# A new planned order for the first 430 operations, with a page model for TensorE's instructions

## The chip, the cores and the metric

The kernel runs on one core of one Trainium2 chip. The metric is device microseconds of one execution, lower is better. Engines are named as the profile names them: PE is TensorE (PEld its weight loads), DVE VectorE, ACT ScalarE, POOL GpSimd, SP SyncE.

## The reference

Two stages, in float32. Attention: for each of 24 chunks of 32 queries, softmax over 8 memory keys and a window of 56 keys, for 4 batches and 8 heads of 64. Then a gated block on x (4 x 768 x 512):

```python
scores = scale * np.matmul(q_c, k_full.transpose(0, 1, 3, 2))   # q_c 32 x 64, k_full 64 x 64
a = np.exp(scores - np.max(scores, axis=-1, keepdims=True))
out[:, :, c_start:c_end] = np.matmul(a / (np.sum(a, -1, keepdims=True) + 1e-09), v_full)
...
h = np.maximum(x @ w_in, 0.0)                  # 512 -> 1024
u, v = h[..., :512], h[..., 512:]
v_n = (v - mean(v)) / np.sqrt(var(v) + 1e-06)
v_s = np.einsum('ts,bsd->btd', w_spatial, v_n) + b_spatial[None, :, None]
out = (u * v_s) @ w_out
```

## The kernel before

The work is cut into 24 attention units of 4 chunks (128 queries, all 8 heads), six to a batch, and into matmul groups of the gated block. A unit i has a burst of small products on PE, `burst`: 64 for the scores and 64 for the weighted values of unit i-1. For units 0 to 3 these are two bursts of 64 (scores, tile sx; values, tile f), from unit 4 on one burst of 128. `softmax` runs on DVE and ACT: `mx` (maximum), `p` (subtraction, then exp), `den`, `rec`. `flip` turns the probabilities (tile pt, copied to pT) and the unit's result xs (tile xt, copied to x); up to unit 8 that is done by PE. `prep` copies the halo of the keys (k from k), before a unit's scores may start.

The gated block's groups (`group`, the matmuls of L901) accumulate in a ring of four PSUM tiles f. Each float32 product is three fp32r products of high and low parts. `ffn_v` and `ffn_u` multiply x by the two halves of w_in, `spatial` by w_spatial (needs the normalised `vn` of all six units of a batch), `ffn_o` by w_out.

w_in and w_out arrive as float64 words. `from_f64` turns each of 12 blocks (8 of w_in, 4 of w_out) into float32 and then into high and low parts, in seven operations: `scale_` (ACT or POOL, L1085 or L1087), `shift` (DVE, L1095), `sign` (DVE, L1101), `high` (ACT or POOL, L386), `rest` (ACT, L1091), `add` (POOL, L1106), `low` (DVE or POOL, L1113).

The order is made by the program itself at build time. Every call of `op` adds an operation with a number, its engine (or a price for each of several engines), its reads and writes and a rank. `Plan.order` is a list scheduler: it walks simulated time, and on each engine takes the operation with the smallest

```python
c = (late + ops[n][10], ops[n][4], n)     # start time + wait, rank, number
```

The table `ORDER` changes single operations by number: (added to the rank, wait, the one engine allowed or ''). Each engine then executes its operations in exactly the planned order, and an operation that waits holds up all behind it on its engine. The loads of SP stand in a queue of their own whose order is that of the list `FIRST` and of the calls; each may start only after the one before it (`after=line`), and at most `AHEAD` bytes of loads are under way.

The table's numbers run in the order of the calls: 0 to 107 are the first loads and the blocks of w_in (14 to 20 block (1,1), 22 block (0,1), 36 block (2,1)); 108 to 117 are unit 0 (110 its `mx`), 133 the key copy of unit 2, 242 to 273 the four blocks of w_out, 274 to 379 `ffn_v` and `ffn_u` of batch 0, and 384 to 429 units 7 to 9 in part.

## Time and profile before

| | us |
|---|---|
| median of 3 runs (lowest, highest) | 381.64 (380.35, 385.66) |
| the profiled execution, its own time | 381.86 |
| its span in the trace | 379.6 |

The span runs from the first to the last instruction that the trace shows; 2.26 us of the execution lie outside it. All rows of the trace below are from that one execution, and their times count from the start of its span. A busy time of PE counts pipelined matmuls, so that neighbours overlap in it.

### The profile page before, as it was taken

Reading aid. Unit: us, or ns where it says so; the run is one execution under the profiler, and the core shown is the slowest. Engines: PE = TensorE matmul, PEld = TensorE weight load, DVE = VectorE, ACT = ScalarE, POOL = GpSimd, SP = SyncE. Lnnn points to the kernel's source line nnn. Section 1 sums busy time; section 2 is a strip of 40 time slices with the busy share of each in tenths; the row PEclk is TensorE's granted clock in tenths of the full one; section 3 lists DMA queues with packets and bytes.
Section 4 is the critical chain, followed back from the end, with each engine's and each line's share of the span. In section 5 each row is a group of like instructions: output and inputs, shape, how many; then the busy total and the mean of one; then the engine's idle time right before and its main releaser. Section 6 shows DMA issues by size and latency. Waiting matters only on the chain.

```text
span 379.6 us, 11226 instructions
## 1 busy us (share of the span) xinstructions
PE 356.5 (94%) x4692; PEld 319.1 (84%) x4692; DVE 204.6 (54%) x408; ACT 253.5 (67%) x659; POOL 151.1 (40%) x230
## 2 busy tenths in 40 slices
PE   1486999989999999999999999999999999999996
PEld 0364898979899889899899889899898889999995
DVE  0777868866437275765546274764555362603030
ACT  4885997862676977877975977879776983411112
POOL 4784786556434323434624323304514410213031
PEclk9999999999999999999999999999999999999999
DMA  6989735971023153134122352124120100000202
GB/s 217 287 301 244 283 98 154 293 233 58 3 86 130 72 147 76 50 79 152 41 87 80 146 126 75 48 60 162 51 86 2 55 29 2 1 0 3 83 0 85
DMA packets 29243, 39.71 MB, mean 105 GB/s; under 512 B 5192, under 2 KB 23304, under 8 KB 29192
## 3 DMA queue, kind: packets, MB, share of 16 engines
q1 hardware_dynamic: 28968, 38.91, 32.7%
q8 instruction: 37, 0.61, 0.7%
q14 instruction: 14, 0.11, 0.1%
q10 hardware_dynamic: 224, 0.08, 0.1%
HBM read 32.69 MB, written 6.29 MB: 103 GB/s over the span
## 4 chain that ended last, share of the span: by engine, by line
PE 82%; ACT 6%; DVE 4%; issue 3%; POOL 2%; DMA 2%; SPq 0%; POOLq 0%; ACTq 0%
PE f L901 71%; PE sx L629 7%; ACT xs L719 2%; POOL st L1087 2%; ACT pT L386 2%; DMA big<-in_moe_w_in_dram 2%; PE pt L818 1%; PE xt L845 1%; PE f L629 1%; DVE mx L743 1%; DVE p L747 1%; ACT big L1020 1%; ACT p L762 1%; DVE vn L963 1%; DVE st L1101 0%
## 5 line engine op out<-in xcount | busy, mean ns | idle before, releaser
L901 PE MATMUL f<-wsp_h,vn 128*128 128x384 f32 x384 | 99.1, 339 | 0.0
L901 PE MATMUL f<-x,win_h 128*128 128x384 f32 x256 | 72.7, 341 | 0.0
L901 PEld LDWEIGHTS f<-wsp_h,vn 128*128 128x128 f32 x384 | 69.3, 188 | 2.6
L901 PE MATMUL f<-wout,big 128*128 128x512 f32 (+1 forms) x300 | 71.4, 382 | 0.0
L901 PE MATMUL f<-wsp_l,vn 128*128 128x384 f32 x192 | 64.5, 336 | 0.0
L719 ACT COPY xs<-sx 32x128 f32<-32x128 f32 x240 | 61.6, 257 | 3.3 <-PE sx L629 0.4
L901 PE MATMUL f<-win_h,x 128*128 128x512 f32 x192 | 63.3, 411 | 0.5 <-ACT x L851 0.2
L901 PEld LDWEIGHTS f<-wout,big 128*128 128x128 f32 x300 | 54.3, 188 | 9.1
L1017 POOL TENSOR_TENSOR st<-st,u 128x384 f32<-128x384 f32 x32 | 33.4, 1044 | 66.2 <-DVE st L1013 45.4
L901 PEld LDWEIGHTS f<-x,win_h 128*128 128x128 f32 x256 | 47.0, 188 | 1.4
L944 POOL TENSOR_TENSOR rstd<-ve,mhalf 128x1 f32<-128x1 f32 x24 | 15.2, 636 | 73.6 <-DVE ve L940 64.5
L386 ACT COPY pT<-p 32x128 f32<-32x128 f32 x144 | 42.6, 296 | 2.3 <-POOL p L798 0.5
L901 PE MATMUL f<-x,win_l 128*128 128x384 f32 x128 | 43.3, 338 | 0.0
L901 PEld LDWEIGHTS f<-win_h,x 128*128 128x128 f32 x192 | 35.4, 193 | 7.7 <-DVE x L855 0.5
L1020 ACT CAST big<-st 128x384 fp32r<-128x384 f32 x32 | 16.4, 512 | 35.8 <-POOL st L1017 35.4
L1013 DVE TENSOR_TENSOR st<-f,bias 128x384 f32<-128x384 f32 x32 | 17.8, 556 | 39.2 <-PE f L901 38.8
L901 PE MATMUL f<-win_l,x 128*128 128x512 f32 x96 | 38.5, 401 | 0.0
L901 PEld LDWEIGHTS f<-wsp_l,vn 128*128 128x128 f32 x192 | 36.1, 188 | 0.0
L1024 DVE TENSOR_TENSOR big<-st,big 128x384 fp32r<-128x384 f32 x32 | 19.4, 605 | 24.8 <-ACT big L1020 24.8
L798 POOL TENSOR_TENSOR p<-p,rec 128x512 f32<-128x512 f32 x15 | 15.7, 1044 | 40.2 <-DVE rec L775 40.2
L386 POOL COPY pT<-p 32x128 f32<-32x128 f32 x96 | 29.8, 310 | 4.4
L629 PEld LDWEIGHTS sx<-k,q 64*32 64x32 f32 x1536 | 17.4, 110 | 14.3 <-POOL k L386 7.9
(91 smaller groups left out, 511.6 us busy)
## 6 DMA issues: line engine op xcount, KB each, us to landing
out_dram<-st SPq DMA_DIRECT2D x23, 256.0 KB
k<-in_k_dram SPq DMA_DIRECT2D x7, 800.0 KB
q<-in_q_dram SPq DMA_DIRECT2D x7, 768.0 KB
vmain<-in_v_dram SPq DMA_DIRECT2D x38, 128.0 KB
vmain<-in_v_dram SPq DMA_DIRECT2D x37, 96.0 KB
big<-in_moe_w_spatial_dram SPq DMA_DIRECT2D x6, 384.0 KB
big<-in_moe_w_in_dram SPq DMA_DIRECT2D x4, 512.0 KB
stage_w<-in_moe_w_in_dram SPq DMA_DIRECT2D x4, 512.0 KB
```

The source lines that it names most:

```text
L386: return (nc.scalar.copy if e == "ACT" else nc.gpsimd.tensor_copy)(o, a).ins
L629: nc.tensor.matmul(o, w_, m, start=start, stop=True, skip_group_check=True)
L719: last_ = (nc.scalar.copy if e == "ACT" else nc.vector.tensor_copy)(o, a).ins
L743: nc.vector.tensor_reduce(mx, s, axis=AX.X, op=ALU.max)
L798: (nc.vector if e == "DVE" else nc.gpsimd).tensor_tensor(p3, p3, rec, op=ALU.mult)
L901: return [nc.tensor.matmul(o, ll if x == 1 else lh, rl if x == 2 else rh, start=x == j == 0, stop=j == len(pairs) - 1 and x == (single[-1] ...
L944: nc.gpsimd.tensor_tensor(a, t_["ve", i], mhalf, op=ALU.pow)
L1013: nc.vector.tensor_tensor(alloc("st", s_, [P, HT], F32), t_["f", n], bias[:, tok], op=ALU.add)
L1017: nc.gpsimd.tensor_tensor(a, a, t_["u", i], op=ALU.mult)
L1020: nc.scalar.copy(t_["g", i][:, 0, 0:HT], t_["st", s_])
L1024: nc.vector.tensor_tensor(a[:, 1, 0:HT], t_["st", s_], a[:, 0, 0:HT].bitcast(F32), op=ALU.subtract)
L1087: nc.gpsimd.tensor_scalar(o, a, 2.0 ** -112, None, op0=ALU.mult)
```

## The change

No operation of the computation is added or taken away. What changes is the order in which the engines execute them, on which of two engines some of them run, and 18 small products that PE executes at the start, into a PSUM tile that nothing reads (`PADS`). The new order follows from four things:

- `ORDER` has 370 entries, for operations 0 to 429, where it had 72 for 5 to 323.
- POOL's prices for `scale_` and `high` of `from_f64` go from 0.75 and 0.7 to 1.5 and 1.0 us.
- A class `Pages` takes the place of the page count: the first matmul instruction is number 67 + 4 x `PADS` in its page, a few instructions in a hundred or a thousand are added to the count, PE's queue is sent up to `DEPTH` instructions ahead of their start, and page n+1 is there `FETCH` after the later of `ASK` past the entry of page n and the landing of the last load begun by then.
- The readiness of an operation by engines other than PE (`others`) limits when its instructions are sent.

The diff, its table cut to lines that the text below speaks of:

```diff
 ORDER = {
-    5: (0, 0, 'ACT'), 6: (21, 3, 'ACT'), 8: (34, 1.5, 'POOL'), 9: (46, 0.4, 'ACT'), 19: (-32, 3, ''),
-    20: (-34, 3, 'DVE'), 22: (22, 0, 'POOL'), 28: (19, 0, 'POOL'), 40: (-20, 0, ''), 48: (27, 0, 'ACT'),
...
+    11: (0, 0.8, ''), 12: (20.6, 0, ''), 13: (-19.7, 0, ''), 14: (36, 0, ''), 15: (26.5, 0.8, ''),
+    16: (12.7, 0.4, ''), 17: (16.5, 0, ''), 18: (9, 0.4, ''), 19: (5.9, 0, ''), 20: (10.7, 6, ''),
+    21: (24.5, 0.8, ''), 22: (40.1, 3, 'POOL'), 23: (-4.6, 0, ''), 24: (-30.7, 0, ''), 25: (77.8, 0, ''),
...
+    34: (-67.3, 6, ''), 35: (70.3, 0.2, ''), 36: (-13.8, 0, 'ACT'), 37: (54.9, 0, ''), 39: (21.1, 0, 'ACT'),
...
+    109: (-20.3, 0.4, ''), 110: (-36.1, 0, ''), 111: (-83.4, 0, ''), 112: (70, 0.4, ''), 113: (-70.7, 0, ''),
...
+    130: (-16.9, 0, ''), 131: (10.6, 0, ''), 132: (61.2, 0.4, ''), 133: (128.8, 0.4, ''), 134: (53.2, 0, ''),
...
+    239: (35.7, 0, ''), 241: (23.6, 0, ''), 242: (-1.8, 0.8, ''), 243: (-46.7, 0, 'ACT'), 244: (-141.6, 0, ''),
+    245: (-14.5, 0, ''), 246: (-59, 0, 'ACT'), 247: (21.4, 0, ''), 248: (17.7, 0, ''), 249: (0.5, 0, ''),
...
+    267: (-72.1, 1.5, 'ACT'), 268: (165, 0, ''), 269: (-0.7, 0, ''), 271: (-16.9, 0, ''), 273: (9, 0, ''),
...
 }
 PAGE = 256
-PADS = 0
+DEPTH = 54
+MORE = (0.009, 2000, 0.0052)
+ASK = 0.95
+PADS = 18
 MARGIN = 0.5
-FETCH = 2.4
+FETCH = 2.6
...
-SCALE = {'ACT': 0.66, 'POOL': 0.75}
-HIGH = {'ACT': 0.6, 'POOL': 0.7}
+SCALE = {'ACT': 0.66, 'POOL': 1.5}
+HIGH = {'ACT': 0.6, 'POOL': 1.0}
...
+class Pages:
+    def __init__(self, first):
+        self.starts, self.sent, self.page, self.first = [], 0.0, 0, first
+        self.there, self.loads = {}, []
+
+    def run(self, ready, t, count, each):
+        at = t
+        for _ in range(count):
+            sent = max(self.sent, ready)
+            if len(self.starts) >= DEPTH:
+                sent = max(sent, self.starts[-DEPTH])
+            n = len(self.starts)
+            page = int((self.first + n + MORE[0] * min(n, MORE[1]) + MORE[2] * max(0, n - MORE[1])) / PAGE)
+            if page != self.page:
+                self.page = page
+                sent = max(sent, self.there.get(page, 0.0))
+                clear = next((end for a, end in reversed(self.loads) if a <= sent + 0.2), 0.0)
+                self.there[page + 1] = max(sent + ASK, clear) + FETCH
+            self.sent = sent
+            at = max(at, sent)
+            self.starts.append(at)
+            at += each
+        return at
...
-                each, first, at = us / count, begun, t
-                for m in range(begun, begun + count):
-                    if m % PAGE == 0:
-                        at = max(at, fetched.get(m // PAGE, 0.0))
-                        fetched[m // PAGE + 1] = max(at, pipe) + FETCH
-                    at += each
-                begun, us = begun + count, at - t
+                at = pages.run(others.get(n, 0.0), t, count, us / count)
+                us = at - t
...
                 pipe = max(pipe, t + us) + moves
+                pages.loads.append((t, pipe))
...
+                    others[m] = max([end[d] + self.lat for d in ops[m][3] if self.on[d] != "PE"], default=0.0)
```

The products of `PADS` are made by lines that the kernel had already:

```python
for _ in range(PADS):
    nc.tensor.matmul(ps_pad[0:CH, 0:2], ident[0:D, 0:CH], ident[0:D, 0:2], start=True, stop=True)
```

## Rows read from the trace of the kernel before

**Rows 1.** The page, part 1: busy time, share of the span, instructions.

```profile
PE 356.5 (94%) x4692; PEld 319.1 (84%) x4692; DVE 204.6 (54%) x408; ACT 253.5 (67%) x659; POOL 151.1 (40%) x230
```

**Rows 2.** The page, part 4: the chain that ended last, by engine.

```profile
PE 82%; ACT 6%; DVE 4%; issue 3%; POOL 2%; DMA 2%; SPq 0%; POOLq 0%; ACTq 0%
```

**Rows 3.** Windows: start:end, length, busy of each engine (instructions), granted clock, DMA share, GB/s.

```profile
0.00:40.00 40.00, 22.16 (x522) 16.41 (x530) 24.53 (x51) 26.81 (x44) 25.43 (x32) 0.96 0.87 262
40.00:78.90 38.90, 38.76 (x809) 34.23 (x795) 29.43 (x62) 33.24 (x60) 27.41 (x23) 1.00 0.64 201
78.90:81.10 2.20, 0.37 (x3) 0.06 (x2) 2.20 (x5) 1.43 (x3) 0.00 (x0) 1.00 0.56 126
81.10:376.70 295.60, 295.20 (x3382) 268.44 (x3382) 148.41 (x293) 191.72 (x553) 98.26 (x175) 1.00 0.22 71
...
36.50:39.90 3.40, 3.40 (x34) 2.67 (x41) 2.89 (x5) 2.12 (x3) 3.25 (x3) 0.56 0.91 284
```

**Rows 4.** Timeline of PE: start, us, operation, count [idle before, releaser].

```profile
5.69 1.18 PE L629 MATMUL sx<-k,q 64*32 64x64 f32 x64 [5.69 <-POOL k L386]
12.98 1.12 PE L818 MATMUL pt<-ident,p 128*128 128x128 f32 x4 [6.11 <-ACT p L762]
...
20.07 1.18 PE L629 MATMUL sx<-k,q 64*32 64x64 f32 x64 [1.83 <-POOL k L386]
...
32.64 0.78 PE L629 MATMUL f<-vmain,pT 64*32 64x64 f32 x49
...
36.49 0.47 PE L629 MATMUL f<-vmain,pT 64*32 64x64 f32 x15 [3.07 <-issue]
...
81.12 0.63 PE L845 MATMUL xt<-ident,xs 128*128 128x128 f32 x4 [1.85 <-DVE xs L694]
```

**Rows 5.** The chain that ended last, pieces in order of time: start, us, what.

```profile
30.42 2.29 PE f L901 x9
...
36.96 1.05 PE pt L818 x4
38.01 1.28 PE f L901 x3
...
47.84 1.41 PE sx L629 x91
...
53.05 0.44 PE pt L818 x4
```

**Rows 6.** The instruction queue, two windows (columns as rows 3), loads, a wait for one.

```profile
q8 instruction: 37, 0.61, 0.7%
...
0.00:33.42 33.42, 18.65 (x474) 13.64 (x475) 19.21 (x42) 22.39 (x38) 20.43 (x28) 1.00 0.86 267
...
0.00:26.20 26.20, 11.90 (x341) 9.08 (x342) 13.95 (x33) 18.22 (x29) 16.97 (x25) 1.00 0.84 271
...
23.22 0.38 SPq L412 DMA_DIRECT2D k<-in_k_dram  x1
26.77 0.82 SPq L412 DMA_DIRECT2D stage_w<-in_moe_w_in_dram  x2
...
28.83 0.51 ACT L386 COPY k<-k 128x384 f32<-128x384 f32 x1 [0.39 <-DMA k<-in_k_dram]
```

**Rows 7.** Timeline of DVE and POOL, 9 to 20 us.

```profile
9.15 0.43 DVE L1095 TENSOR_SCALAR st<-st 128x512 uint32<-128x512 uint32 x1 [7.77 <-POOL st L1087]
...
10.85 0.69 DVE L743 TENSOR_REDUCE mx<-sx 128x8 f32<-128x512 f32 x1
...
18.06 1.51 POOL L1087 TENSOR_SCALAR st<-big 128x512 f32<-128x512 f32 x1
...
19.52 0.50 POOL L386 COPY k<-k 128x384 f32<-128x384 f32 x1
```

**Rows 8.** Groups by line: scale_ on POOL and on ACT, count, busy, mean ns, idle before.

```profile
L1087 POOL TENSOR_SCALAR st<-big 128x512 f32<-128x512 f32 x6 | 9.4, 1569 | 5.5 <-DMA big<-in_moe_w_out_dram 3.8 <-DMA big<-in_moe_w_in_dram 1.5 <-DVE shift L952 0.3
...
L1085 ACT ACTIVATE stage_z<-stage_w 128x512 f32<-128x512 f32 x4 | 2.7, 668 | 3.1 <-DMA stage_w<-in_moe_w_in_dram 3.1
```

## The prediction

> **What bounds the kernel now.** I read the page first: PE is busy for 94% of the span [rows 1], and the chain that ended last runs through PE for 82% of it [rows 2]. A share over the whole span hides where the rest lies, so I cut the span into stretches next [rows 3]. From 81.10 to 376.70 us PE is busy for 295.20 of 295.60 us. Nothing that an order does can be won there; only the time at which that stretch begins can move. From 40.00 to 78.90 us PE is busy for 38.76 of 38.90. What is lost lies in two places: in the first 40 us PE is busy for 22.16, and 1.85 us are lost just before 81.12 [rows 3, 4]. The first 40 us are bound by arrival: the DMA engines are busy for 0.87 of them. The order of the loads is fixed by the program's list and isn't in the diff, so most of that loss stays whatever is done. The timeline of PE then gives each wait with its releaser [rows 4]: 5.69 us for the first keys, 6.11 for unit 0's softmax, 1.83 for a copy of keys on POOL, 3.07 for "issue", that is for nothing that another engine or a load of data releases, and 1.85 for xs on DVE.

> **The stall of 3.07 us.** It stands inside a burst whose 64 products need the same data: 49 run at 32.64, the other 15 at 36.49 [rows 4]. So no operand was late, and instructions are what remains. The instruction queue moved 0.61 MB in 37 packets [rows 6]: 16.5 KB each, and 9384 matmuls and weight loads over 37 are 254 to a packet, against a page of 256 in the code. Up to the stall PE had started 474 matmuls and 475 weight loads [rows 6], 949 instructions. With the diff's 67 before them and its 0.009 for each, 949 + 67 + 8.5 = 1024.5, the fourth multiple of 256. The page edge stands where the stall is.

> Why was this page late? By the same count page 3 was entered 256 instructions earlier: by 26.20 us 341 + 342 had started [rows 6], which is 683 + 67 + 6 = 756 of 768. So the next page was asked for from about 26.4 us on, and came 10 us later. Two loads of w_in, 1 MB together, were issued at 26.77 [rows 6], with the DMA engines busy for 0.86 of that time.

> The 18 products move the count by 72 instructions, 36 products. With the order of before, page 3 would be entered after about 311 products in place of 347, inside the burst of values of unit 1 near 24 us. The next page would be asked for ahead of the loads of 26.77, with the key load of 23.22 still under way; that one had landed by 28.83 [rows 6]. Some 2 to 3 us later, by an estimate from the lag of 36.49 behind 33.42, would be 32 us, about when it is needed. The new PE order moves this again, and can't be seen from a trace of the old one; but an order chosen with these edges in the count has no reason to keep a stall of this size.

> With the stall goes what it did to the clock. PE stood still from 33.42 to 36.49, and from 36.50 to 39.90 the granted clock is 0.56 in the mean, mostly the lower of the two levels [rows 3]. The price, pair by pair against the same work at full clock [rows 5]: 15 small products 0.47 - 15 x 1.41/128 = 0.30; four transposes 1.05 - 0.44 = 0.61; three products of 512 columns 1.28 - 3 x 2.29/9 = 0.52. Sum 1.43. **Term A: 3.07 + 1.43 = 4.50 us.**

> [...]

> **The softmax of unit 0.** Its scores are done at 5.69 + 1.18 = 6.87 us, and mx starts at 10.85 [rows 4, 7]: 3.98 us late. DVE was idle for 7.77 us, held by a shift of w_in that stood ahead of mx and waited for POOL's scale_. The old plan took 0.75 us for scale_ on POOL; the trace has 1.57 in the mean and 0.67 on ACT [rows 8]. The new table moves mx (110) forward and that shift (15) back, and the price is now 1.5. Likewise the keys of unit 2 were copied by POOL at 19.52, behind a scale_ of 1.51 [rows 7], while PE waited 1.83 [rows 4]; that scale_ (36) goes to ACT. **Term B** lies between 0 (PE waits for parts of w_in in this stretch anyhow, and for v) and 3.98 us. The nearest row is PE's own wait of 1.83; I take half of it, 0.9, because PE is so far from being filled there that an earlier burst partly ends in an earlier wait.

> **The wait at 79 us.** PE has nothing to do until DVE delivers xs of unit 7 [rows 4]; DVE is busy for all 2.20 us of that window [rows 3]. If PE comes there 5.4 us earlier and the other engines do not, the whole gain is given back here. **Term C** is between +1.85 (the wait goes) and -5.4. On the one side, w_out's data, for which POOL waits 3.8 us in its queue [rows 8], doesn't come earlier by itself. On the other, its conversion isn't needed by xs, and the new table takes scale_ of two of its four blocks to ACT (243, 267) and reorders units 7 and 8. I take 0, the wait as the row has it.

> **Moved and added work.** Six scale_ are on POOL now, 9.4 us [rows 8]; if half go to ACT, ACT has 2.0 us more and POOL 4.7 less. ACT is at 33.24 of 38.90 us in the second stretch [rows 3], so that stretch has 5.7 us of cover; without it each scale_ would cost 0.67. The 18 products lie in the first 5.69 us, where PE waits for keys: 36 passes at 1.18/64 us are 0.66 us, or, by the dearer row of the transposes, 1.12/4, 10 us [rows 4]. I take 0.66, whose weights have the same shape, and nothing of it shows under a wait of 5.69; at 10 us the first scores would start some 4 us late or more, which is as much as the rival that gives the gain back. SP's queue has the same loads in the same order; a load that waits for a buffer is issued when a conversion has freed it, earlier if scale_ is quicker.

> **The sum.** 4.50 + 0.9 + 0 = 5.4 us. Against the profiled execution, 381.86 - 5.4 = 376.46; the median of the runs is 0.22 lower, so 376.2 us.

> **The rivals.**

> - *More is won.* With B at 3.98 and C at +1.85 the gain is 10.33 and the time 371.3. For it: five times as many entries, all in the stretch that is lost. Against it: the DMA engines at 0.87 are the floor under the first 40 us.
> - *The gain is given back.* C eats A and B: 381.6. For it: DVE is full at the wait of 79 us, and w_out lands when it lands. It would show as a longer wait of PE between 60 and 85 us. A half of this gives 379.
> - *The stall isn't the page's.* Then the page model does nothing, A stays, and only B is won: 380.7. Against it: the count to 1024.5.
> - *Slower: two late pages in place of one.* If the new order runs two bursts, a full page, within the 10 us that a page took here while loads were queued, PE stands still again. It decides when a page is needed sooner than the loads ahead of it land; two such stalls at A's price give 381.6 + 4.5 = 386.1.

> **How the numbers follow.** 2% of this kernel, 7.6 us, is about what a measurement can tell from no change. My forecast, 374.0 to 378.5, has 0.45. More won, under 374.0, has 0.25. Given back has 0.17 and the other cause 0.05, together 378.5 to 383. Slower by late pages has 0.05, and another 0.03 goes to something worse, over 389.3. Faster by over 2% is below 374.0: 0.25; slower by over 2%: 0.03; within: 0.72. The range from 371.0 to 382.0 takes in the bounds of B and C upward and the gain given back, and leaves out the late pages and half of what is worse or better than any row.

> **What the new profile would show.** A right: no "issue" wait of PE above 1 us in the first 45 us, and the granted clock at full there once PE is filled. B right: mx of unit 0 within 1 us of the end of its scores, and no key copy behind a scale_. C right: a wait of about 1.9 us near 74 us. From there to the end the stretch should be as long as now, 296 us and the tail; if it is longer, late pages or waits in later bursts have come in, and the prediction is wrong for that reason. It is also wrong if PE dries out twice between 60 and 85 us.

## The result and the profile after

| | before | after |
|---|---|---|
| median, us (lowest, highest; runs) | 381.53 (380.35, 385.66; 4) | 377.62 (377.31, 378.57; 4) |
| the profiled execution | 381.86 | 377.31 |
| its span | 379.6 | 375.5 |

The ratio is 0.9892, with an interval from 0.9855 to 0.9928: about 1.1% less, 3.9 us between the medians and 4.1 us between the spans. The forecast of 376.2 was 1.4 us too low.

Page of the kernel after, parts 1, 3 and 4, to hold against [rows 1, 2] and the first of [rows 6].

```profile
PE 359.0 (96%) x4728; PEld 321.3 (86%) x4728; DVE 210.2 (56%) x408; ACT 251.0 (67%) x651; POOL 147.5 (39%) x238
...
q8 instruction: 37, 0.61, 0.7%
...
PE 91%; DMA 7%; POOL 1%; DVE 0%; SPq 0%; ACT 0%; issue 0%
```

The chain now runs through PE for 91% where it was 82%, and "issue" is down from 3% to 0. The instruction queue still brings 37 packets, 0.61 MB. The 36 more matmuls of PE (x4728, in [rows 1] x4692) are the 18 products, for each of which the trace has two: x36 at 1.41 us in the timeline below.

Windows of the kernel after (columns as in [rows 3]), the first four answering to those of before.

```profile
0.00:40.00 40.00, 26.75 (x544) 20.14 (x545) 26.36 (x50) 28.76 (x50) 24.00 (x30) 0.83 0.89 271
40.00:78.90 38.90, 38.90 (x817) 34.78 (x816) 32.28 (x70) 34.54 (x64) 23.11 (x20) 1.00 0.68 196
78.90:81.10 2.20, 2.20 (x16) 2.16 (x15) 1.93 (x5) 2.20 (x6) 0.96 (x3) 1.00 0.94 260
81.10:372.60 291.50, 291.14 (x3357) 264.19 (x3355) 149.67 (x285) 185.14 (x534) 99.39 (x187) 1.00 0.22 70
21.00:30.30 9.30, 6.11 (x140) 4.34 (x140) 9.13 (x16) 6.92 (x15) 4.35 (x5) 0.50 0.89 268
30.30:35.20 4.90, 4.89 (x134) 3.62 (x134) 2.08 (x3) 3.54 (x7) 4.49 (x5) 0.57 0.95 243
```

PE is full from 40.00 to 81.10, so the wait near 79 us is gone. But its 26.75 busy us in the first 40, against 22.16 in [rows 3], are not 4.6 us more work: the granted clock is 0.50 from 21.00 to 30.30 and 0.57 from 30.30 to 35.20 (0.50 up to 34.40 and 1.00 from 34.70, in finer windows), and a product counts longer there: 64 small ones take 1.18 us at 21.14 and 1.17 at 30.31, against 0.86 at 41.05, where the clock reads 1.00. A busy column can only be read beside the clock column.

Timeline of PE of the kernel after (columns as in [rows 4]).

```profile
1.41 2.07 PE L450 MATMUL xt<-ident 64*32 64x2 f32 x36 [1.41 <-POOL ident masks.py:199]
5.53 1.19 PE L718 MATMUL sx<-k,q 64*32 64x64 f32 x64 [2.04 <-POOL k L475]
9.58 1.11 PE L907 MATMUL pt<-ident,p 128*128 128x128 f32 x4 [2.87 <-ACT p L851]
...
20.44 0.77 PE L907 MATMUL pt<-ident,p 128*128 128x128 f32 x4 [2.11 <-ACT p L851]
21.14 1.18 PE L718 MATMUL sx<-k,q 64*32 64x64 f32 x64
23.05 1.28 PE L718 MATMUL f<-vmain,pT 64*32 64x64 f32 x64 [0.73 <-issue]
25.82 1.12 PE L907 MATMUL pt<-ident,p 128*128 128x128 f32 x4 [1.49 <-ACT p L851]
...
30.31 1.17 PE L718 MATMUL sx<-k,q 64*32 64x64 f32 x64 [0.59 <-ACT k L475]
...
34.26 1.04 PE L718 MATMUL f<-vmain,pT 64*32 64x64 f32 x64
...
41.05 0.86 PE L718 MATMUL sx<-k,q 64*32 64x64 f32 x64
```

The burst of values at 34.26 runs all its 64 products in one piece; in [rows 4] it was 49, a stall of 3.07 us, and 15. After 30.31 nothing keeps PE waiting until near the end. The softmax of unit 0 is 3.4 us earlier (its probabilities are transposed at 9.58, in [rows 4] at 12.98), but unit 2's scores start at 21.14, 1.1 us later than the 20.07 of [rows 4].

Timeline of DVE and ACT of the kernel after, to hold against [rows 7].

```profile
7.01 0.69 DVE L832 TENSOR_REDUCE mx<-sx 128x8 f32<-128x512 f32 x1
...
17.03 0.69 DVE L836 TENSOR_TENSOR p<-sx,mx 128x512 f32<-128x512 f32 x1
...
17.57 0.83 ACT L666 COPY vmain<-vmain 24x768 f32<-24x768 f32 x1
18.91 0.83 ACT L666 COPY vmain<-vmain 24x768 f32<-24x768 f32 x1 [0.50 <-DMA vmain<-in_v_dram]
19.76 0.63 ACT L851 ACTIVATE p<-p 128x512 f32<-128x512 f32 x1
20.29 0.50 ACT L475 COPY k<-k 128x384 f32<-128x384 f32 x1
```

Unit 0's mx no longer stands behind a shift: 7.01, where it was 10.85. Unit 1 pays for it. Its p is ready on DVE at 17.72, but the exp on ACT stands behind two copies of v, the second of which waits 0.50 us for a load, and runs at 19.76. In before it ran 1 us sooner, as ACT's timeline there has it:

```profile
18.77 0.63 ACT L762 ACTIVATE p<-p 128x512 f32<-128x512 f32 x1
```

And PE takes unit 1's transposes ahead of unit 2's scores in after (20.44, then 21.14), where before has unit 2's scores first (20.07), so these scores wait for unit 1's p too.

**Where the 4 us came from.** The busy column won't do, so I count the products that PE has begun by four times and price each at full clock, from rows of stretches where the granted clock reads 1.00 [rows 3, 6]. The prices come from rows of before that did not stand ahead of the prediction, in the timeline of PE:

```profile
42.84 0.64 PE L901 MATMUL f<-win_h,x 128*128 128x512 f32 x2
...
43.54 0.62 PE L901 MATMUL f<-win_h,x 128*128 128x512 f32 x2
...
49.65 0.51 PE L901 MATMUL f<-x,win_h 128*128 128x384 f32 x2
...
50.17 0.52 PE L901 MATMUL f<-x,win_h 128*128 128x384 f32 x2
```

From each of these rows to the next of its kind three products are begun, as one lies between them: 0.70 us from 42.84 to 43.54, so 0.233 for one of 512 columns, and 0.52 from 49.65 to 50.17, so about 0.175 for one of 384. A small product is 1.41/128 = 0.011 and a transpose 0.44/4 = 0.11 [rows 5]. The 18 products are left out of the counts:

| by | before: 512, 384, small, transposes | us of work | after | us of work | after is ahead by |
|---|---|---|---|---|---|
| 20 us | 0, 0, 192, 8 | 2.99 | 6, 0, 192, 8 | 4.39 | +1.4 |
| 30 us | 12, 0, 363, 20 | 8.99 | 9, 0, 320, 20 | 7.82 | -1.2 |
| 40 us | 24, 0, 470, 28 | 13.84 | 30, 2, 448, 28 | 15.35 | +1.5 |
| 81.1 us | 72, 90, 1088, 60 | 51.10 | 72, 109, 1088, 68 | 55.31 | +4.2 |

So after is ahead by 1.4 us at 20 us, has lost that and 1.2 more by 30, won 2.7 from 30 to 40 and another 2.7 from 40 to 81.1. From there to the end nothing changes: 4.2 ahead against 4.1 in the span.

### The profile page after: what moved, and what is told of

Its sections match the earlier page's. It is cut to its first block, busy times and chain, and to the rows that moved or that the text cites. A ratio compares the mean times of both kernels' runs of the same rounds, so it can differ in the third digit from the quotient of the medians.

```text
span 375.5 us, 11305 instructions
## 1 busy us (share of the span) xinstructions
PE 359.0 (96%) x4728; PEld 321.3 (86%) x4728; DVE 210.2 (56%) x408; ACT 251.0 (67%) x651; POOL 147.5 (39%) x238
## 3 DMA queue, kind: packets, MB, share of 16 engines
q1 hardware_dynamic: 28968, 38.91, 33.5%
## 4 chain that ended last, share of the span: by engine, by line
PE 91%; DMA 7%; POOL 1%; DVE 0%; SPq 0%; ACT 0%; issue 0%
PE f L990 81%; PE sx L718 8%; DMA vmain<-in_v_dram 2%; DMA stage_w<-in_moe_w_in_dram 2%; DMA big<-in_moe_w_in_dram 2%; DMA k<-in_k_dram 2%; PE xt L934 1%; PE pt L907 1%; POOL st L1176 0%; SPq L501 0%; DVE big L1113 0%; PE f L718 0%; POOL v L475 0%; ACT big L1109 0%; ACT k L475 0%
## 5 line engine op out<-in xcount | busy, mean ns | idle before, releaser
L1106 POOL TENSOR_TENSOR st<-st,u 128x384 f32<-128x384 f32 x32 | 34.3, 1076 | 71.5 <-DVE st L1102 64.8
L1033 POOL TENSOR_TENSOR rstd<-ve,mhalf 128x1 f32<-128x1 f32 x24 | 16.5, 687 | 66.3 <-DVE ve L1029 48.9
L475 ACT COPY pT<-p 32x128 f32<-32x128 f32 x128 | 37.9, 296 | 2.5 <-POOL p L887 1.0
L990 PE MATMUL f<-win_l,x 128*128 128x512 f32 x96 | 38.7, 403 | 0.0
L475 POOL COPY pT<-p 32x128 f32<-32x128 f32 x112 | 33.9, 303 | 5.0
L1113 DVE TENSOR_TENSOR big<-st,big 128x384 fp32r<-128x384 f32 x32 | 21.7, 679 | 16.7 <-ACT big L1109 16.1
L851 ACT ACTIVATE p<-p 128x512 f32<-128x512 f32 x24 | 15.1, 629 | 21.4 <-DVE p L836 21.3
```

The lines of the kernel that those rows point to most:

```text
L475: return (nc.scalar.copy if e == "ACT" else nc.gpsimd.tensor_copy)(o, a).ins
L851: nc.scalar.activation(p3, p3, AF.Exp, scale=scale)
L990: return [nc.tensor.matmul(o, ll if x == 1 else lh, rl if x == 2 else rh, start=x == j == 0, stop=j == len(pairs) - 1 and x == (single[-1] ...
L1033: nc.gpsimd.tensor_tensor(a, t_["ve", i], mhalf, op=ALU.pow)
L1106: nc.gpsimd.tensor_tensor(a, a, t_["u", i], op=ALU.mult)
L1113: nc.vector.tensor_tensor(a[:, 1, 0:HT], t_["st", s_], a[:, 0, 0:HT].bitcast(F32), op=ALU.subtract)
```

## The experiments

The theory going in was the prediction's: the stall is a page of instructions that comes late, and the order with the pages counted avoids it. Its rivals were that the stall has another cause, that a gain there is given back later, and that the time comes from the order alone, whatever the pages.

**The old order with its page edges moved.** The plan of before does not count the 18 products, so `PADS` moves the edges and leaves the order as it was. A second kernel has 3 in place of 18.

```diff
-PADS = 0
+PADS = 18
```

> The kernel before with the 18 products ahead and nothing else: the same order on every engine, 72 instructions more at the start. Page theory: the edge moves 36 products forward, from 49 products into the burst of values of unit 2 to about 13 into it, and the page before it is entered inside the burst of values of unit 1, ahead of the loads of w_in issued near 26.8 us; so the issue wait of 3.07 us falls to under 1 us. Whether the time falls with it tells what the wait near 79 us does: if PE is the bound from 40 us on, the time falls by 3 to 4.5 us, to 377 to 378.5; if DVE and w_out are, the wait near 79 us grows from 1.85 to 4 to 6 us and the time stays at 381 to 382. Rival, the stall has another cause than a page: it stays at 3.07 us between the same two products, and so does the time.

> The kernel before with 3 products ahead, 12 instructions, 6 products' worth. Page theory: the page is still asked for after the loads of 26.8 us, so the issue wait stays at 2.5 to 3.5 us, but it stands 6 products earlier in the same burst: 43 and 21 in place of 49 and 15. Rival, another cause: 49 and 15 as before.

Measured with 18: 381.91 us (10 runs), ratio 1.0002 (0.9969 to 1.0035). With 3: 382.36 (one run). Timeline of PE with 3:

```profile
32.64 0.68 PE L629 MATMUL f<-vmain,pT 64*32 64x64 f32 x43
...
35.12 0.42 PE L629 MATMUL f<-vmain,pT 64*32 64x64 f32 x21 [1.81 <-issue]
```

And with 18, in its shortest run:

```profile
32.78 0.94 PE L629 MATMUL f<-vmain,pT 64*32 64x64 f32 x64
34.86 0.66 PE L818 MATMUL pt<-ident,p 128*128 128x128 f32 x4 [1.14 <-ACT p L762]
...
78.70 0.63 PE L845 MATMUL xt<-ident,xs 128*128 128x128 f32 x4 [1.28 <-DVE xs L694]
```

Three idle products are 12 instructions, 6 of the burst's, and the cut in the burst moved from 49 | 15 to 43 | 21, product for product. Nothing else was touched, so the stall is at a page edge: that theory is shown. The stall itself is shorter than the 2.5 to 3.5 us expected, and a wait of 2.31 us for p follows it at 37.85, which [rows 4] doesn't have. With 18 the stall is gone, and the time is the same. What the prediction called "given back" happens in the old order, though not as I expected: the wait near 79 us doesn't grow to 4 to 6 us, it is 1.28 in this trace.

**The new order with its page edges moved.** The idle products are taken out, while the plan goes on counting them, so the order is that of after.

```diff
-PADS = 18
+PADS = 0
-Pages(67 + 4 * PADS)
+Pages(67 + 4 * 18)
```

> The kernel after with its order kept word for word and the 18 products left out. Page theory: page 4 begins 36 products later, at about product 474 of the rest, near the end of the burst of values of unit 2 at 34 us, and is asked for near 28.6 us, behind the loads issued at 26.1 and 29.8 us; an issue wait of 1 to 3 us comes back there, and the time is 1 to 3 us longer, 378.5 to 380.5. Rival, the products only stand there and the order alone made the gain: no issue wait above 0.8 us and 377.6.

Measured: 388.29 us (4 runs), ratio 1.0153 (1.0114 to 1.0192), outside both expectations: 10.7 us above the median of after, and some 10 by the two ratios. Timeline of PE:

```profile
33.63 0.83 PE L718 MATMUL f<-vmain,pT 64*32 64x64 f32 x55
37.54 0.44 PE L718 MATMUL f<-vmain,pT 64*32 64x64 f32 x9 [3.08 <-issue]
...
74.90 0.63 PE L718 MATMUL sx<-vmain,pT 64*32 64x64 f32 x19 [3.49 <-issue]
```

The stall is back, 3.08 us, behind the same 474th product as in before, and a second of 3.49 us stands in unit 7's burst, behind 2220 instructions: with the diff's 67, 0.009 for each of the first 2000 and 0.0052 for each of the rest that is 2306, against 9 x 256 = 2304. So a late page was worth much more here than I had priced it: besides two stalls, 6.6 us, the granted clock is lower behind each (0.82 in the mean from 40.00 to 50.00 us, 0.50 from 75.00 to 79.00). Unit 4's burst starts at 46.30, against 41.05 in after: 5.2 us for one stall and what follows from it. From unit 7's burst to unit 8's PE takes 13.9 us (70.09 to 84.01), where it takes 7.4 in after (64.83 to 72.24): 6.5 us for the other. Together they are the 11.8 us between the two spans, 387.3 and 375.5.

**One part of the change alone.** Three kernels take the change apart: after with the table of before; after with the entries from 242 on taken out (units 7 to 9, w_out and batch 0's groups), so that only units 0 to 6 and w_in keep their entries; and before, with its old page count and prices, with the table of after. The cut below is of the first two; in the third, before's 72 entries give way to after's 370.

```diff
 ORDER = {
-    0: (117.6, 6, ''), 1: (1.7, 0, ''), ...        (after's 370 entries)
+    5: (0, 0, 'ACT'), 6: (21, 3, 'ACT'), ...       (before's 72, or after's below 242)
```

> The kernel after (page model, new prices, 18 products) with the old table of 72 entries, so that the order is a third one. If the gain comes from the page model and the prices, most of it is here: 378 to 379. If it comes from the searched entries, which fit this model alone, little or nothing is: 381 or more, with waits of PE between 20 and 85 us other than those of either kernel.

> The kernel after without the table's entries from 242 on, that is without those for w_out, for the groups of the gated block of batch 0 and for units 7 to 9. The order of attention units 0 to 6 and of w_in keeps its entries, though groups that fill PE between them change. Theory, these entries removed the wait near 79 us: PE waits of 1 to 3 us come back between 60 and 85 us, 379 to 381. Rival, that wait went by itself when PE's stall near 33 us did: no such wait, 377 to 378.

> The kernel before (old page count, old prices, no products ahead) with the new table of 370 entries. If the table is a better order by itself: 378 to 380. If it fits the model that it was searched with and nothing else, as the old table under the new plan did at 399.8: 388 to 400, with waits of PE in the first 45 us and an issue wait of 1 to 4 us.

Measured: 399.82 (ratio 1.0449, 1.0379 to 1.0519), 393.46 (1.0333, 1.0283 to 1.0384) and 397.12 (1.0400, 1.0368 to 1.0432), 4 runs each. All are slower than before by 3% to 4.5%; the first and the third are as the second theory of each expected, and the cut table is outside both of its expectations. The waits of PE, summed by what ended them, in after with the old table:

```profile
PE sx L657 <- ACT k L414: 8.3, 1, 8.3
PE xt L873 <- DVE xs L722: 3.8, 2, 3.0
```

in after with the cut table:

```profile
PE pt L1047 <- ACT p L991: 9.4, 7, 3.0
PE sx L858 <- issue: 3.1, 3, 1.9
```

and in before with the new table:

```profile
PE pt L879 <- ACT p L823: 8.7, 4, 3.5
...
PE xt L906 <- DVE xs L760: 5.4, 3, 3.2
```

A table of ranks belongs to the plan that it was made for. With other prices or another page count the same entries give another order, with keys, p or xs late. These three kernels therefore don't share out the gain among table, prices and pages; they show that none of these parts gave a gain without the others.

**What took the stall's place in the old order.** The kernel with 18 idle products was run again for a second trace, as the first came from its shortest run. Then the plan was told that w_out's four loads land 3 us later than it reckons, which changes the order of the engines only from about 66 us on.

> The kernel before with 18 products ahead once more, for a second trace: the first came from the shortest of ten runs, 379.5 us, while the median was 381.9. If the stall's time is given back by waits on other engines, a run of 381 to 383 us has no issue wait above 1 us and 2 to 4 us more of waits of PE on DVE and ACT between 33 and 85 us, or a stretch of lower clock there. If the stall comes back in such runs, an issue wait of 2 to 3 us stands in the burst of values of unit 2.

```diff
-PAGE = 256
+PAGE, LATE = 256, {242: 3.0, 250: 3.0, 258: 3.0, 266: 3.0}
...
-                end[n] = pipe + self.landing
+                end[n] = pipe + self.landing + LATE.get(n, 0.0)
```

> The kernel before with 18 products ahead, as in the two runs of that name, and its plan told that the four blocks of w_out land 3 us later than it took them to. The order of each engine stays the same up to about 66 us; there POOL computes the rstd of the last units ahead of its first scale_ of w_out in place of behind it, and w_out's conversion goes behind the softmax of unit 8 and xs of unit 7 in part. Theory, the wait near 79 us (1.3 and 2.5 us in the two traces with 18 products) is made by engines held in their order by w_out: it falls under 1 us and the time to 378.5 to 380.5, which is the gain of the stall no longer given back. Rival, units 7 and 8 have the wait for reasons of their own: it stays, and 381 to 383.

The first took 383.70 us (one run). Its timeline of POOL, DVE and PE, in order of time:

```profile
69.23 1.53 POOL L1087 TENSOR_SCALAR st<-big 128x512 f32<-128x512 f32 x1 [4.40 <-DMA big<-in_moe_w_out_dram]
70.72 0.58 POOL L944 TENSOR_TENSOR rstd<-ve,mhalf 128x1 f32<-128x1 f32 x1
...
71.33 0.60 DVE L952 SCALAR_TENSOR_TENSOR shift<-mvar,rstd 128x1 f32<-128x1 f32 x1 [1.77 <-POOL rstd L944]
...
80.39 0.63 PE L845 MATMUL xt<-ident,xs 128*128 128x128 f32 x4 [2.46 <-DVE xs L694]
```

This run has no stall in the burst of values either. The wait at 80 us grows to 2.46 us and its chain can be read down these lines: POOL waits 4.40 us for w_out and does scale_ first, because the plan put that ahead; rstd, which was wanted, comes at 70.72; DVE waits 1.77 for it, and so does all that DVE has to do before xs.

That wait isn't all that this run lost. xs's transposes still start 0.73 us earlier than in [rows 4], and yet the span is 381.5 us, 1.9 longer than before's. A window (columns as in [rows 3]) and a line of PE's timeline have the rest:

```profile
81.00:84.00 3.00, 3.00 (x13) 2.90 (x12) 1.97 (x4) 1.15 (x3) 2.11 (x3) 0.50 1.05 397
```

```profile
280.92 0.21 PE L629 MATMUL sx<-vmain,p 64*32 64x64 f32 x1 [1.19 <-issue]
```

Behind the wait the granted clock is 0.50 for 3 us, and unit 9's burst starts at 91.35, in before at 90.52: the lead is gone. Then one more page is late, which I had not expected: the last product of a burst waits 1.19 us, behind 8081 instructions, by the same count 8198 against 32 x 256 = 8192. The next burst is 1.85 us behind that of before (292.41, 290.56), and so is the end.

With the later landing told to the plan, the timeline of POOL and PE is:

```profile
68.95 0.55 POOL L944 TENSOR_TENSOR rstd<-ve,mhalf 128x1 f32<-128x1 f32 x1 [2.33 <-DVE ve L940]
69.47 1.92 POOL L1087 TENSOR_SCALAR st<-big 128x512 f32<-128x512 f32 x1
...
77.97 0.60 PE L845 MATMUL xt<-ident,xs 128*128 128x128 f32 x4
```

rstd now goes first, and PE no longer waits for xs. Measured: 380.31 us (10 runs), ratio 0.9968 (0.9938 to 0.9998) against 1.0002 for the kernel without the edit: some 0.3%, its interval just off no change, and overlapping that of the kernel without the edit. So by the traces the wait for xs is a part of what ate the stall's gain in the old order, and not all of it: the trace of this kernel has a wait of 3.36 us for p before 37.37. What taking the wait for xs away is worth in time isn't shown apart from nothing.

**After with the clock held.** Eighteen idle products of 512 columns are put where PE waits in after: 8 and 6 before the transposes of units 1 and 2, 4 before unit 1's values. Nine of the idle products of the start are taken out for them, so that the page edges stay. The same kernel was run twice, the second time beside after itself on one chip.

```diff
+WARM = {1: 8, 2: 6}
+WARM_P = {2: 4}
+WARM_N = sum(WARM.values()) + sum(WARM_P.values())
...
-    for _ in range(PADS):
+    for _ in range(PADS - WARM_N // 2):
...
+                    for _ in range(WARM_P.get(i, 0)):
...
+                for _ in range(WARM.get(i, 0)):
+                    nc.tensor.matmul(a, minus, minus.unsqueeze(1).broadcast_to([P, T, P]), start=True, stop=True,
+                                     skip_group_check=True)
```

> The kernel after with 18 products of 512 columns added that nothing reads, in places where PE stands still between 18 and 26 us: 8 ahead of the transposes of unit 1, 4 ahead of the values of unit 1, 6 ahead of the transposes of unit 2; 9 of the 18 products at the start are taken out, so that the page edges behind them stay where they are. The order is the same. After's PE works without a wait from 30.3 us on, but its clock is at the lower level until about 34.9 us: 4.9 us for what takes 2.9 at the higher. Theory, that clock costs time at the end: the granted clock stays up from 18 us, the same work is done 1.5 to 2 us earlier, and 375.6 to 376.5 us come out. Rival, the parts of w_in and the keys set the pace there whatever the clock is: PE gets waits in place of slow work, and the time stays at 377 to 378.

> The kernel after once more, beside the next one on the same chip: 377.0 to 378.5, ratio 0.987 to 0.992, and a spread of under 2 us, as in its first runs.

> The kernel after with the 18 idle products against the lower clock, once more, beside the kernel after on the same chip. If holding the clock is worth its 2 us at the end in most runs: 375 to 376.5 and at least 1 us under the kernel after. If the earlier PE runs into late pages or operands in many of its runs, as its first spread of 374.7 to 381.5 suggests: 376.5 to 378, within 1 us of the kernel after, with the wider spread.

Measured: 377.12 us (12 runs, 374.70 to 381.49), ratio 0.9873 (0.9845 to 0.9901); then 376.68 (6 runs, 374.45 to 378.36), 0.9859 (0.9826 to 0.9891), beside after with 377.48 (6 runs, 375.27 to 379.75), 0.9882 (0.9848 to 0.9916). That is the rival's side of the first and of the last expectation; after's own spread is 4.5 us, where I expected under 2. Windows, and then a line of PE's timeline, of the first of these runs:

```profile
20.00:30.00 10.00, 8.74 (x223) 6.65 (x223) 9.35 (x16) 8.27 (x18) 4.79 (x6) 1.00 0.95 306
30.00:40.00 10.00, 9.82 (x228) 7.41 (x211) 8.67 (x17) 9.27 (x17) 7.98 (x8) 1.00 0.94 250
```

```profile
38.95 0.86 PE L721 MATMUL sx<-k,q 64*32 64x64 f32 x64
```

Windows of after in its second profile, and a line of PE's timeline there:

```profile
20.00:30.00 10.00, 5.08 (x178) 3.57 (x178) 9.10 (x16) 8.58 (x18) 5.54 (x6) 1.00 0.92 302
30.00:40.00 10.00, 10.00 (x153) 7.59 (x130) 7.12 (x14) 8.46 (x15) 6.67 (x7) 0.83 0.93 259
```

```profile
21.45 0.86 PE L718 MATMUL sx<-k,q 64*32 64x64 f32 x64
```

A line of PE's timeline in the second profile of the kernel with the clock held:

```profile
19.15 0.62 PE L999 MATMUL f<-win_h,x 128*128 128x512 f32 x2 [1.21 <-issue]
```

With the idle products the granted clock reads 1.00 over both windows, unit 4's burst starts at 38.95 where after's first profile has 41.05, and that trace's span is 2.1 us shorter. But after itself doesn't always lose the clock so early: in its second profile it is at 1.00 from 20 to 30 us and 0.83 from 30 to 40, and its span is 374.5. Unit 2's scores bear the column out: 0.86 us there, 1.18 in the first profile. And the kernel with the clock held doesn't always keep what it wins: in its second profile PE waits 1.21 us at 19.15 behind 443 instructions, by the count 514 against 2 x 256 = 512, a late page where the first profile has no wait; the span is 375.0. On one chip, beside each other, the two kernels differ by 0.8 us in the median with overlapping intervals. The lower clock in after's first profile, 0.50 from 21.00 to 34.40 us, is real; that holding the clock is worth anything in the median isn't shown. No kernel here is shown to beat after.

## Why the prediction came out right, point by point

**The stall is the page's: right.** 43 | 21 with 3 idle products and 55 | 9 in the new order without them put the cut where the count puts it. The packets of before's instruction queue bear it out. By the count pages 1 and 2 are entered near 15.1 and 20.3 us, and a packet begins near 16.9 and 23.0, 1.8 and 2.7 us later; page 4 is entered at 36.49, and a packet begins near 38.7. Page 3 is entered between 27.2 and 28.0 us by the same count, where the prediction has 26.4, and no packet begins until 33.5, over 5 us later; the stall ends 3 us behind that. Of the 37 packets of before it is the only one with a stall of this kind: 3.07 us. Its like are the 1.81, 3.08 and 3.49 us in the kernels with the edges moved, and the 1.19 and 1.21 of the later traces.

**Term A, 4.50 us: the stall was right, the clock and so the size was not.** The window from 30 to 40 us won 2.7 us. The 3.07 of stall went. The 1.43 of slow clock did not: I expected the full level "once PE is filled", and in after PE is filled from 30.31 on at 0.50 until 34.40, and at 1.00 from 34.70. (The 0.56 of [rows 3] is 0.50 from 36.20 to 39.40 and 1.00 from 39.60 on.) I had tied the lower clock to the stall alone; in after it came without one, with the waits of 2.11 and 1.49 us on p around its fall. From 30.30 to 35.20 PE began 128 small products and 6 of 512 columns: 2.8 us at the full-clock prices, where it took 4.9, so some 2.1 us went there.

**Term B, +0.9 us: it came, and was lost again.** Both things that it rested on came true: mx is 3.8 us earlier, and unit 2's keys are copied by ACT with no scale_ ahead, though not sooner (20.29, where [rows 7] has 19.52). By 20 us after is ahead by 1.4 us. The step that failed is that a lead there stays won, with PE's own wait of 1.83, halved, for the stretch: by 30 us after has done 1.2 us less work than before. PE got other waits for it, 1.49 on unit 2's p and 0.73 for "issue", and the lower clock. About half is the clock's: in after's second profile, where it is at 1.00 from 20 to 30 us, PE has begun 10 products of 512 columns, 354 small ones and 20 transposes by 30 us, 8.4 us of work and 0.6 less than before. The bound from below should have gone under 0. That unit 1's exp behind the copies of v is where the rest begins is read from the rows above; no run tried it.

**Term C, 0: it was +2.7.** The step that failed is "the wait as the row has it". After has no wait near 79 us. The idle time that went is 0.14 + 1.85 = 2.0 us of the 2.7 [rows 3, 4]; the other 0.7 isn't itemised by any row here, and lies within what the prices of the count can be off. I had the end +1.85 in the range, and the right reason for it: that conversion isn't needed by xs. In the trace with w_out told as later the wait is gone with rstd put first, so that link is what held xs in the old order. Which entries of the new table cut it was not tried apart; the cut table, which lacks them all, has other waits in their place.

**The sum was 5.4, it came to 4.2:** -1.2 + 2.7 + 2.7, where 0.9 + 4.5 + 0 was said. The terms were off by -2.1, -1.8 and +2.7, and these cancelled: that the total came so near is luck. What vouches for A's mechanism is the kernels with the edges moved, not the total.

**The rivals.** "The gain is given back" is false of after and true of the old order with its edges moved, 381.91: the stall's gain alone is worth nothing there. "More is won" had C at its upper end, which came, and B at its own, which didn't. "Slower: two late pages" is what the new order without its idle products does, at 388.29 by more than the price I gave. Both together say what the change is: an order and page edges that fit one another.

**Moved and added work** cost nothing, as said, but both sizes were off. The 18 products took 2.07 us, three times the 0.66 that I took, all under the wait for the first keys: the first scores start at 5.53, in [rows 4] at 5.69. Five of POOL's six scale_ went to ACT, not three; ACT is at 34.54 of 38.90 us in the second stretch.

**The rest** is as long as said: 291.5 us from 81.10, with after 4.2 us ahead there, and the tail; no late page after 81 us in this trace, where PE's longest wait is 0.3 us, on DVE.

**Left open:** which table entries end the wait at 79 us; why the clock falls at another time in two profiles of after; and why a page is late in one execution and not in another of the same kernel, which is a part of the spread of the old order with 18 products, 379.52 to 384.21. That the loads under way make a page late is argued from the DMA shares: no run moved a load alone. And no table was searched with the old page count, so whether such an order could be found without the page model isn't known.

## What to carry to other kernels

When a burst of identical products breaks in the middle and the wait is called "issue", count the instructions before it: if the cut stands on a multiple of the page, 256 by the count here, put a few idle instructions ahead. A change of their number that moves the cut by as many, as 12 moved it by 6 products here, shows that it is the page's. Not every "issue" is one: the 0.73 us at 23.05 in after stands behind 621 instructions, 694 by the count, far from 512 and 768, and its cause is open. Price the stall by undoing it, not by its length: it was worth nothing in one order and 5.2 and 6.5 us in another, since the waits next in line and the clock decided. Count work at full-clock prices rather than busy time when the granted clock differs, and take a planned order's ranks, prices and page count as one piece.

## What the runs showed that was not expected

- Of the 37 pages one was found late in before (3.07 us), none in after, and two in the new order without its idle products (3.08 and 3.49), each while data was moving: while PE stood still the DMA engines were busy for 0.92 of the time in before, and for 0.92 and 0.82 in the new order without its idle products. From 10 to 20 us in the kernel with the clock held, where the page at 19.15 is late, their share reads 1.02. From 81 us on, with a DMA share of 0.22, neither before nor after has a late page in its profile; the one at 280.92 in the old order with 18 products shows that a page can be late there too.
- Taking out 18 products whose result nobody reads cost some 10 us.
- The granted clock reads 1.00 in the first 20 us, and yet 64 small products take 1.19 us there (5.53) against 0.86 later (41.05), as they do at 21.14 where it reads 0.50 (1.18). So the column doesn't seem to show the clock of the start of an execution.
- Two profiles of one kernel, after, differ in when PE's clock falls: 0.50 and 0.57 between 21 and 35 us in the one, 1.00 up to 30 us and 0.83 from 30 to 40 in the other.
